# Smaller feed-forward units for the first block, a mean square in halves, a new order of loads, and a new load model in the scheduler of a fused attention and SwiGLU kernel

## The chip, the cores and the metric

The kernel runs on one core of a Trainium2 chip. The metric is the device time of one execution in microseconds (us). Each group of runs times the kernel before beside the kernels under test on the same chip. A ratio is the mean time of one kernel's fast runs over that of the other kernel's fast runs of the same rounds, so it is not quite the ratio of the medians quoted beside it. Its 95% interval is in brackets.

## The reference

Sliding-window attention (128 positions and 4 sink positions) over 4 batches, 8 heads, 768 positions, head size 64. Then each of the 3072 tokens goes through a root mean square normalisation and a SwiGLU feed-forward network (FFN).

```python
keep = is_sink | ((rel >= 0) & (rel < window))            # n_sink 4, window 128
a = softmax(where(keep, q @ k.T / sqrt(D), -1e9))
x = (a @ v).transpose(0, 2, 1, 3).reshape(B * S, H * D)   # 3072 x 512
xn = x / sqrt(mean(x * x, -1) + 1e-6) * rms_g
g = xn @ w_gate                                           # 512 x 1536
out = (g * sigmoid(g) * (xn @ w_val)) @ w_out             # 1536 x 512
```

## The kernel before

The tokens form 24 blocks of 128 rows; four blocks form a group. The 1536 FFN columns are 12 tiles of 128, called weight tiles here; "gate 2-3" means tiles 2 and 3 of the gate weights, "value 2-3" the same of the value weights. All loads except three at the start go through one software queue that GpSimd issues; it casts float32 to bfloat16 on the way.

Nothing is issued in program order. Each operation is registered with a cost in ns, what it needs and what it gives. A list scheduler (`Plan.run`) plays a model of the engines, the PSUM banks and the loads, and emits instructions in the order in which they start there. (PSUM is the memory that TensorE writes its products to; a bank is a piece of it that a product holds until it has been read.) Each engine then executes in that order and waits at the head of its queue.

```python
def land(self, ring, first, work):          # the scheduler's model of a load
    r = self.rings
    if ring == "POOL":                      # software queue
        begin = max(first, r["POOL"], r["HW"])
        r["POOL"] = begin + (1.4 * work if begin < 8500 else work)
        self.loads -= 1
        return r["POOL"] + 520
    if ring == "HW":                        # two float32 blocks and the gains, from SyncE
        begin = max(first, r["HW"])
        r["HW"] = begin + (1.25 * work if begin > 2500 else work)
        return r["HW"] + 900
    # ... transposes and stores cut
```

```python
LOADS = ("q-1 k-1 v-0 w-0-2 v-1 qkv-2 qkv-3 w-2-4 w-4-6 w-6-8 w-8-9 w-9-12 qkv-4 "
         "wo-0-6 qkv-5 wo-6-12 qkv-6 qkv-8 qkv-7")      # one literal in the source
LOADS += "".join(f" qkv-{g}" for g in range(9, NB))
WARM = 30             # products of zeros that fill TensorE's gaps
PE_MASKS = 2          # blocks masked by a product on TensorE, not on VectorE
CHUNKS = (4, 2, 2)    # group 0: one block of rows at a time, 4 weight tiles a unit

def square(g):        # mean square of a block, one ScalarE instruction
    nc.scalar.activation(out=sq, in_=T["x16", g].rearrange("p h d -> p (h d)"),
        func=ACT.Square, scale=1.0 / math.sqrt(DM), accum_out=T["ms", g])

def ffn(G, n, fts, cols, prio):             # one unit; banks and most needs cut
    pe(864, lambda: mms(bank(("g", key)), wg, G, fts, cols), ...)   # gate product
    pe(864, lambda: mms(bank(("v", key)), wv, G, fts, cols), ...)   # value product
    act(480, lambda: tanh(key), ...)
    dve(600, lambda: silu(key), ...)
    dve(605, lambda: hidden(key, G, fts, cols), ...)

for G in range(NG):
    nc_ = CHUNKS[G] if G < len(CHUNKS) else 1
    w, n = GN // nc_, 0
    for c in range(nc_):
        for ft in range(0, FTN, nc_):
            ffn(G, n, range(ft, ft + nc_), slice(c * w, (c + 1) * w), p0 + 10 * n)
            n += 1
```

The softmax here doesn't subtract the row's maximum and nothing guards it: scores larger than these inputs give would overflow.

Of the kernel before, what the change touches and what calls it, by code (L numbers as in the profile page):

```python
# [9 lines left out]
ALU = mybir.AluOpType  # L10
ACT = mybir.ActivationFunctionType
FP32 = mybir.dt.float32
# [14 lines left out]
class Plan:  # L27
# [3 lines left out]


    LATE = 300
    HOP = {"PE": 40, "ACT": 35, "DVE": 35, "POOL": 90, "SP": 60}
    START = {"PE": 800, "ACT": 800, "DVE": 1030, "POOL": 1290, "SP": 800}

# [5 lines left out]
    def op(self, ways, needs=(), gives=(), prio=0.0, takes=(), drops=(), ring=None, work=0.0,  # L42
# [3 lines left out]
            drops=tuple(drops), ring=ring, work=work, mode=mode, at=len(self.ops), ready=0,  # L46
        ))

    def land(self, ring, first, work):


        r = self.rings
        if ring == "POOL":
            begin = max(first, r["POOL"], r["HW"])
            r["POOL"] = begin + (1.4 * work if begin < 8500 else work)
            self.loads -= 1
            return r["POOL"] + 520
        if ring == "HW":
            begin = max(first, r["HW"])
            r["HW"] = begin + (1.25 * work if begin > 2500 else work)  # L60
            return r["HW"] + 900
        begin = max(first, r["TR"], r["POOL"])
        if self.loads:
            r["POOL"] = max(r["POOL"], first) + work
            work *= 2
        r["TR"] = begin + work
        return r["TR"] + (350 if ring == "TR" else 650)

    def run(self):
        free, users = dict(self.START), {}  # L70
        self.loads = sum(o["ring"] == "POOL" for o in self.ops)
        wait = {o["at"]: set(o["needs"]) for o in self.ops}
        cand = {e: [] for e in free}
        left = len(self.ops)
        for o in self.ops:
            for t in o["needs"]:
                users.setdefault(t, []).append(o)
            if not o["needs"]:
                for e in o["ways"]:
                    cand[e].append(o)  # L80
        busy, warm, mode, order = [], False, 0, []
        while left:
            first = None
            for e, found in cand.items():
                for o in found:
                    k = len(o["takes"])
                    if k > len(self.banks):
                        continue
                    ready = o["ready"] + self.HOP[e] if o["ready"] else 0
                    if k:  # L90
                        ready = max(ready, sorted(self.banks.values())[k - 1] + 40)
                    start = max(free[e], ready)
                    key = (start, o["prio"], ready, o["at"])
                    if first is None or key < first[0]:
                        first = key, e, o
            if first is None:
                raise RuntimeError("stuck: %s" % [
                    (o["gives"], list(wait[o["at"]])) for o in self.ops if o["at"] in wait
                ][:20])
            (start, *_), e, o = first  # L100
            for x in o["ways"]:
                cand[x].remove(o)
            wait.pop(o["at"])
            left -= 1
            ns, lat, fn = o["ways"][e]
            if e == "PE":
                busy = [(a, d) for a, d in busy if a > start - 3413]
                warm = start - free[e] < 4000 and (warm or sum(d for a, d in busy) > 3000)
                ns = ns if warm else 2 * ns
                if o["mode"] != mode:  # L110
                    ns, mode = ns + 110, o["mode"]
                busy.append((start, ns if mode != 2 else 0))
                lat = ns + 180
            for s in o["takes"]:
                i = min(self.banks, key=lambda i: (self.banks[i], i))
                del self.banks[i]
                self.held[s] = i
            free[e] = start + ns
            end = start + lat
            if o["ring"] is not None:  # L120
                end = self.land(o["ring"], end, o["work"]) + self.LATE
            for s in o["drops"]:
                self.banks[self.held[s]] = end + 12
            for t in o["gives"]:
                for x in users.pop(t, ()):
                    x["ready"] = max(x["ready"], end + 12)
                    w = wait[x["at"]]
                    w.discard(t)
                    if not w:
                        for way in x["ways"]:  # L130
                            cand[way].append(x)
            order.append((start, end, e, fn, o))
        return order
# [3 lines left out]
def kernel(  # L137
# [34 lines left out]
    GROW = "SP"  # L172
    CAST_DVE = 600
    MASKS_PRIO = -5
    POOL_AT = (1,2)
    DEPTH = 8
    LOADS = "q-1 k-1 v-0 w-0-2 v-1 qkv-2 qkv-3 w-2-4 w-4-6 w-6-8 w-8-9 w-9-12 qkv-4 wo-0-6 qkv-5 wo-6-12 qkv-6 qkv-8 qkv-7"
    LOADS += "".join(f" qkv-{g}" for g in range(9, NB))
    PE_MASKS = 2
    POOL_MASK_FROM = 16  # L180
    X_DMA_FROM = 9
    QK_DMA_FROM = 8
    LD = 16
    GATE_FROM = 6
    LOAD_LEAD = 9
    LEAD_FROM = 10
    WARM = 30
    GATE_LEAD = 6
    T_LEAD = 3
    SPLIT = (0,1)  # L190
    CHUNKS = (4,2,2)
    GB_PRIO = 2000

    const = ctx.enter_context(tc.tile_pool(name="const", bufs=1))
    ld = ctx.enter_context(tc.tile_pool(name="ld", bufs=LD))
# [330 lines left out]
    def normal(g, u):  # L526
# [7 lines left out]
            in1=rden.unsqueeze(2).to_broadcast((P, 4, D)), op=ALU.mult,  # L534
        )

    def square(g):
        T["ms", g] = small.tile([P, 1], FP32, name="ms")
        sq = xpool.tile([P, DM], BF16, name="sq")
        nc.scalar.activation(  # L540
            out=sq, in_=T["x16", g].rearrange("p h d -> p (h d)"), func=ACT.Square,
            scale=1.0 / math.sqrt(DM), accum_out=T["ms", g],
        )

    def rms(g):
        m = small.tile([P, 1], FP32, name="m")
        nc.vector.tensor_scalar(
            out=m, in0=T.pop(("ms", g)), scalar1=1e-6, scalar2=None, op0=ALU.add,
        )
        y = small.tile([P, 1], FP32, name="y")  # L550
        nc.vector.tensor_scalar(
            out=y.bitcast(I32), in0=m.bitcast(I32), scalar1=-0.5,
# [94 lines left out]
    for g in range(NB):  # L647
# [41 lines left out]
        for u in range(2):  # L689
# [7 lines left out]
            else:  # L697
# [12 lines left out]
            dve(548, lambda g=g, u=u: normal(g, u),  # L710
                [("av", g, u)] + ([("xr", g - 3)] if g >= 3 else [])
                + ([("n", g - 1, u)] if g else []), [("n", g, u)], early, drops=[("av", g, u)])
        act(720, lambda g=g: square(g),
            [("n", g, 0), ("n", g, 1), "table"] + ([("ms", g - 1)] if g else []), [("ms", g)],
            early)
        dve(1745, lambda g=g: rms(g),
            [("ms", g), "gb"] + ([("xt", g - 3)] if g >= 3 else [])
            + ([("xr", g - 1)] if g else []), [("xr", g)], early)
# [34 lines left out]
    def mms(ps, w_sb, G, fts, cols):  # L753
        n = cols.stop - cols.start
        for i, ft in enumerate(fts):
            for kt in range(KTN):
# [2 lines left out]
                    rhs=T["xnt", G][:, kt, cols], start=(kt == 0), stop=(kt == KTN - 1),  # L759
                )  # L760

    def tanh(key):
        T["th", key] = spool.tile([P, 512], BF16, name="th")
        nc.scalar.activation(  # L764
            out=T["th", key], in_=BANK[("g", key)], func=ACT.Tanh, scale=0.5,
        )

    def silu(key):
        T["p1", key] = spool.tile([P, 512], BF16, name="p1")
        nc.vector.scalar_tensor_tensor(  # L770
            out=T["p1", key], in0=T.pop(("th", key)), scalar=1.0, in1=BANK.pop(("g", key)),
            op0=ALU.add, op1=ALU.mult,
        )

    def hidden(key, G, fts, cols):
        n, hk = len(fts), ("h", G, fts[0] // 4)
        if hk not in T:
            T[hk] = hpool.tile([P, 4, GN], BF16, name="hT")
        i = fts[0] % 4
        nc.vector.tensor_tensor(  # L780
            out=T[hk][:, i:i + n, cols],
            in0=T.pop(("p1", key)).rearrange("p (n c) -> p n c", n=n),
            in1=BANK.pop(("v", key)).rearrange("p (n c) -> p n c", n=n), op=ALU.mult,
        )

    def project(G, tb, i):
# [45 lines left out]
    def ffn(G, n, fts, cols, prio):  # L832
        key = (G, fts[0], cols.start)
        xs = [("xt", g) for g in range(G * GB + cols.start // P, G * GB + cols.stop // P)]
        before = [("h", keys[-3])] if len(keys) >= 3 else []
        keys.append(key)
        pe(864, lambda: mms(bank(("g", key)), wg, G, fts, cols),
           xs + [("wg", ft) for ft in fts], [("g", key)], prio, takes=[("g", key)])
        pe(864, lambda: mms(bank(("v", key)), wv, G, fts, cols),
           [("g", key)] + [("wv", ft) for ft in fts], [("u", key), ("F", G, n)], prio - 0.5,  # L840
           takes=[("v", key)])
        act(480, lambda: tanh(key), [("g", key), "table"] + before, [("th", key)])
        dve(600, lambda: silu(key), [("th", key)] + before, [("p1", key)], drops=[("g", key)])
        dve(605, lambda: hidden(key, G, fts, cols), [("p1", key), ("u", key)]
            + ([("O", G - 2, i) for i in range(GB)] if G >= 2 else []),
            [("h", key)], drops=[("v", key)])

    for G in range(NG):
# [1 line left out]
        nc_ = CHUNKS[G] if G < len(CHUNKS) else 1  # L850
        w, n = GN // nc_, 0
        for c in range(nc_):
            for ft in range(0, FTN, nc_):
                ffn(G, n, range(ft, ft + nc_), slice(c * w, (c + 1) * w), p0 + 10 * n)
                n += 1
        mine = [key for key in keys if key[0] == G]
        for tb in range(GB if G < NG - 1 else GB - 1):
# [61 lines left out]
```

## Time and profile before

| | before |
|---|---|
| median of 3 runs | 246.89 us (246.82 to 247.07) |
| span of the profiled execution | 244.3 us (that run took 245.98 us, the fastest of its group) |
| TensorE (PE) busy | 232.6 us, 95% |
| VectorE / ScalarE busy | 183.7 / 131.2 us |
| granted TensorE clock, mean | 0.999 |

The page of the kernel before. The first line is busy time with its share of the span and the number of instructions, by engine. The others divide the span into 40 slices of about 6 us: each digit is the busy share of a slice in tenths, and GB/s is what the DMA engines moved.

```profile
PE 232.6 (95%) x2098; PEld 147.8 (61%) x2120; DVE 183.7 (75%) x482; ACT 131.2 (54%) x276; POOL 88.8 (36%) x114
...
PE   4978999999999999999999999999999999999994
...
GB/s 112 172 170 195 192 188 188 156 146 174 171 196 130 156 124 179 142 216 133 149 35 107 133 107 86 3 21 108 120 34 21 4 21 107 86 3 0 0 86 86
```

TensorE is short of full only in the first, third and fourth slice and in the last; the loads run at a steady 170 to 195 GB/s from the second slice to the seventh. After the fourth slice the engine is dense. What can be won is TensorE work done earlier in the first 25 us.

The timeline of TensorE around the first FFN products (kernel before; columns: start us, length us, engine, line, operation, output and inputs, shapes, count; in brackets the idle time just before it and what ended it):

```profile
18.14 0.61 PE L757 MATMUL g<-xnt,wg 128*128 128x128 bf16 x8
19.75 0.62 PE L757 MATMUL g<-xnt,wg 128*128 128x128 bf16 x8 [1.00 <-DMA wg<-in_moe_w_gate_dram]
...
20.49 1.06 PE L757 MATMUL v<-xnt,wv 128*128 128x128 bf16 x16
...
22.09 1.06 PE L757 MATMUL g<-xnt,wg 128*128 128x128 bf16 x16
22.98 1.06 PE L757 MATMUL v<-xnt,wv 128*128 128x128 bf16 x16
23.88 0.61 PE L757 MATMUL g<-xnt,wg 128*128 128x128 bf16 x8
24.68 0.51 PE L757 MATMUL g<-xnt,wg 128*128 128x128 bf16 x6 [0.19 <-DMA wg<-in_moe_w_gate_dram]
```

Eight gate products run at 18.14. Then TensorE stands for 1.00 us until gate 2-3 has landed. From 19.75 it works almost without a gap.

### The profile page before, as it was taken

What the parts mean: (1) busy time and instruction counts of PE and PEld (TensorE: products, weight loads), DVE (VectorE), ACT (ScalarE), POOL (GpSimd) and SP (SyncE); (2) the same over time, 40 slices, a digit from 0 to 9 for tenths busy, and PEclk for the clock granted to TensorE, in tenths of its full rate; (3) what the DMA queues carried; (4) which work ended last, traced back from release to release, by engine and by line L of the source; (5) the groups of instructions that cost most, each with busy time, mean ns of one, the idle gap of its engine ahead of it and who ended that gap; (6) DMA issues with size and microseconds to landing.
All of it is one profiled execution on the core that took longest, in us unless ns stands there. A gap on an engine that the chain in (4) does not pass through costs nothing.

```text
span 244.3 us, 5510 instructions
## 1 busy us (share of the span) xinstructions
PE 232.6 (95%) x2098; PEld 147.8 (61%) x2120; DVE 183.7 (75%) x482; ACT 131.2 (54%) x276; POOL 88.8 (36%) x114
## 2 busy tenths in 40 slices
PE   4978999999999999999999999999999999999994
PEld 2557996875789765688875444444545544444443
DVE  4388979979899998899888499991299992377700
ACT  3886466778675837654537555735745521333111
POOL 8995755695444749423004200302504200000000
PEclk9999999999999999999999999999999999999999
DMA  8999999999999999999944544014311013200022
GB/s 112 172 170 195 192 188 188 156 146 174 171 196 130 156 124 179 142 216 133 149 35 107 133 107 86 3 21 108 120 34 21 4 21 107 86 3 0 0 86 86
DMA packets 111979, 27.22 MB, mean 111 GB/s; under 512 B 102097, under 2 KB 109009, under 8 KB 111954
## 3 DMA queue, kind: packets, MB, share of 16 engines
q0 software_dynamic: 80704, 13.90, 81.0%
q1 hardware_dynamic: 31106, 12.85, 27.0%
q8 instruction: 16, 0.26, 0.5%
q10 hardware_dynamic: 144, 0.13, 0.2%
q14 instruction: 9, 0.07, 0.1%
HBM read 28.31 MB, written 6.29 MB: 142 GB/s over the span
## 4 chain that ended last, share of the span: by engine, by line
PE 77%; DVE 9%; POOL 5%; DMA 4%; issue 3%; ACT 0%; POOLq 0%; DVEq 0%; ACTq 0%
PE o L790 23%; PE g L757 21%; PE v L757 21%; PE s L456 4%; DMA wg<-in_moe_w_gate_dram 4%; DVE hT L780 2%; PE av L520 2%; DVE p L770 2%; PE av L515 2%; DVE r L560 2%; POOL v L327 1%; DVE xr L564 1%; PE av L505 1%; PE o_last L808 1%; DVE x L532 1%
## 5 line engine op out<-in xcount | busy, mean ns | idle before, releaser
L757 PE MATMUL g<-xnt,wg 128*128 128x128 bf16 (+2 forms) x525 | 69.8, 282 | 1.6 <-DMA wg<-in_moe_w_gate_dram 1.2
L757 PE MATMUL v<-xnt,wv 128*128 128x128 bf16 (+2 forms) x522 | 71.0, 281 | 0.3
L764 ACT ACTIVATE th<-g 128x512 bf16<-128x512 f32 x72 | 42.9, 600 | 46.7 <-PE g L757 45.2
L790 PE MATMUL o<-wo,hT 128*128 128x512 bf16 x263 | 62.6, 379 | 1.2 <-issue 0.6
L770 DVE SCALAR_TENSOR_TENSOR p<-th,g 128x512 bf16<-128x512 bf16 x72 | 48.1, 683 | 16.6 <-ACT th L764 16.2
L757 PEld LDWEIGHTS <-wg 128*128 128x128 bf16 x528 | 43.1, 98 | 21.0 <-DMA wg<-in_moe_w_gate_dram 1.5
L757 PEld LDWEIGHTS <-wv 128*128 128x128 bf16 x528 | 42.6, 98 | 18.5 <-issue 0.8
L469 ACT ACTIVATE e<-s 128x512 bf16<-128x512 f32 (+1 forms) x104 | 48.4, 542 | 6.6 <-PE s L456 6.3
L780 DVE TENSOR_TENSOR hT<-p,v 128x512 bf16<-128x512 bf16 x72 | 47.2, 682 | 1.5 <-PE v L757 0.6
L790 PEld LDWEIGHTS <-hT 128*128 128x128 bf16 x276 | 25.6, 98 | 28.7 <-issue 1.3
L491 POOL TENSOR_SCALAR_AFFINE_SELECT e<-e 128x512 bf16<-128x512 bf16 x14 | 9.4, 680 | 61.8 <-ACT e L469 48.8
L798 ACT ACTIVATE osb<-o 128x512 f32<-128x512 f32 x23 | 13.8, 599 | 29.0 <-PE o L790 29.0
L323 POOL DMA_DIRECT2D k<-in_k_dram x23 | 20.5, 890 | 15.9 <-DMA v<-in_v_dram 7.0
L323 POOL DMA_DIRECT2D q<-in_q_dram x23 | 20.5, 893 | 13.0 <-DMA k<-in_k_dram 3.8
L327 POOL DMA_DIRECT2D v<-in_v_dram x24 | 21.3, 889 | 10.0 <-DMA q<-in_q_dram 6.0
L532 DVE TENSOR_TENSOR x<-av,rden 128x256 bf16<-128x256 f32 x48 | 20.4, 425 | 1.7
L540 ACT ACTIVATE sq<-x 128x512 bf16<-128x512 bf16 x24 | 15.2, 632 | 9.4 <-DVE x L532 9.3
L531 DVE RECIPROCAL rden<-av 128x4 f32<-128x4 f32 x48 | 8.5, 177 | 15.4 <-PE av L520 15.3
L486 DVE TENSOR_TENSOR e<-e,masks 128x1024 bf16<-128x1024 bf16 (+1 forms) x30 | 18.9, 650 | 1.0 <-ACT e L469 0.8
L564 DVE SCALAR_TENSOR_TENSOR xr<-x,r,gb 128x512 bf16<-128x512 bf16 x24 | 19.0, 790 | 0.9
L520 PE MATMUL av<-v,e 128*128 128x65 bf16 x192 | 16.9, 194 | 0.0
L515 PE MATMUL av<-v,e 128*128 128x65 bf16 x160 | 15.0, 193 | 0.0
(70 smaller groups left out, 177.2 us busy)
## 6 DMA issues: line engine op xcount, KB each, us to landing
out_dram<-osb SPq DMA_DIRECT2D x23, 256.0 KB, 2.2
v<-in_v_dram POOLq DMA_DIRECT2D x24, 128.0 KB, 10.4
q<-in_q_dram POOLq DMA_DIRECT2D x23, 128.0 KB, 10.9
k<-in_k_dram POOLq DMA_DIRECT2D x23, 128.0 KB, 10.8
wo<-in_moe_w_out_dram POOLq DMA_DIRECT2D x2, 768.0 KB, 12.0
wg<-in_moe_w_gate_dram POOLq DMA_DIRECT2D x4, 256.0 KB, 7.8
wv<-in_moe_w_val_dram POOLq DMA_DIRECT2D x4, 256.0 KB, 8.2
wg<-in_moe_w_gate_dram POOLq DMA_DIRECT2D x1, 384.0 KB, 9.4
```

What stands on the lines that cost most here:

```text
L323: nc.gpsimd.dma_start(out=T[name, g], in_=block_of(src, g))
L327: nc.gpsimd.dma_start(out=V16[b][:, t, :, 0:D], in_=block_of(v, g))
L469: nc.scalar.activation(out=T["e", g, u][:, 2 * hi:2 * hi + 2, n0:n1, :].rearrange("p x n c -> p x (n c)"), in_=ps.rearrange("p (j c) -> p ...
L515: nc.tensor.matmul(out=dest, lhsT=T["e", g - 1, u][:, x, 1, :], rhs=V16[b][:, t - 1, h, :], start=(t == 1), stop=False, skip_group_check=True,
L520: nc.tensor.matmul(out=dest, lhsT=T["e", g, u][:, x, 0, :], rhs=V16[b][:, t, h, :], start=(t == 0), stop=True, skip_group_check=True,)
L532: nc.vector.tensor_tensor(out=T["x16", g][:, 4 * u:4 * u + 4, :], in0=pvv[:, :, 0:D], in1=rden.unsqueeze(2).to_broadcast((P, 4, D)), op=AL ...
L564: nc.vector.scalar_tensor_tensor(out=T["xr", g], in0=T.pop(("x16", g)).rearrange("p h d -> p (h d)"), scalar=r[:, 3:4], in1=gb, op0=ALU.mu ...
L757: nc.tensor.matmul(out=ps[:, i * n:(i + 1) * n], lhsT=w_sb[:, kt, ft * P:(ft + 1) * P], rhs=T["xnt", G][:, kt, cols], start=(kt == 0), sto ...
L764: nc.scalar.activation(out=T["th", key], in_=BANK[("g", key)], func=ACT.Tanh, scale=0.5,)
L770: nc.vector.scalar_tensor_tensor(out=T["p1", key], in0=T.pop(("th", key)), scalar=1.0, in1=BANK.pop(("g", key)), op0=ALU.add, op1=ALU.mult,)
L780: nc.vector.tensor_tensor(out=T[hk][:, i:i + n, cols], in0=T.pop(("p1", key)).rearrange("p (n c) -> p n c", n=n), in1=BANK.pop(("v", key)) ...
L790: nc.tensor.matmul(out=BANK[("o", G, tb)], lhsT=T["h", G, ft // 4][:, ft % 4, tb * P:(tb + 1) * P], rhs=wo[:, ft, :], start=(ft == 0), sto ...
```

## The change

The intent: start the FFN of block 0 as soon as two weight tiles are there, shorten the path from attention to normalised rows for blocks 0 and 1, and let the scheduler model hardware and software loads as sharing the DMA engines. Several settings of the scheduler move with it, among them the order and sizes of the loads and the number of warm-up products.

```diff
-            begin = max(first, r["POOL"], r["HW"])
-            r["POOL"] = begin + (1.4 * work if begin < 8500 else work)
+            begin = max(first, r["POOL"])
+            self.soft = min(self.soft, begin)
+            r["POOL"] = self.end(begin, work, ((r["HW"], 0.25), (7000, 0.7)))
 ...
-            begin = max(first, r["HW"])
-            r["HW"] = begin + (1.25 * work if begin > 2500 else work)
+            begin = max(first + (300 if r["HW"] else 0), r["HW"])
+            r["HW"] = self.end(begin, work, ((self.soft, 1.05), (1e9, 0.38)))
 ...                       (a SLACK table of zeros, which changes nothing, cut)
-    POOL_AT = (1,2)
+    POOL_AT = (0,1)
-    LOADS = "q-1 k-1 v-0 w-0-2 v-1 qkv-2 qkv-3 w-2-4 w-4-6 w-6-8 w-8-9 w-9-12 qkv-4 wo-0-6 qkv-5 wo-6-12 qkv-6 qkv-8 qkv-7"
+    LOADS = "q-1 k-1 v-0 v-1 qkv-2 w-0-2 qkv-3 w-2-4 w-4-6 w-6-9 w-9-10 w-11-12 w-10-11 qkv-4 wo-0-6 qkv-5 wo-6-12 qkv-8 qkv-7 qkv-6"
-    PE_MASKS = 2
+    PE_MASKS = 3
-    GATE_FROM = 6
+    GATE_FROM = 7
-    LEAD_FROM = 10
-    WARM = 30
+    LEAD_FROM = 9
+    WARM = 0
+    FIRST = 2
+    SQ2 = 2
-    GB_PRIO = 2000
+    GB_PRIO = -970
 ...
+    def square_half(g, u):        # for blocks 0 and 1; rms() adds the two halves
+        cols = slice(u * DM // 2, (u + 1) * DM // 2)
+        nc.scalar.activation(
+            out=T["sq", g][:, cols], in_=T["x16", g].rearrange("p h d -> p (h d)")[:, cols],
+            func=ACT.Square, scale=1.0 / math.sqrt(DM), accum_out=T["ms", g][:, u:u + 1],
+        )
 ...                       (unit size and its costs passed through ffn, cut)
-            for ft in range(0, FTN, nc_):
-                ffn(G, n, range(ft, ft + nc_), slice(c * w, (c + 1) * w), p0 + 10 * n)
+            k = min(nc_, FIRST) if G == 0 and c == 0 else nc_
+            for ft in range(0, FTN, k):
+                ffn(G, n, range(ft, ft + k), slice(c * w, (c + 1) * w), p0 + 10 * n)
```

In `LOADS`, `w-6-9` is one load of weight tiles 6 to 8 for the gate and one for the value weights. `FIRST` is the number of weight tiles in a unit of block 0 (a unit is the gate and the value product of some tiles for some rows, with the steps behind them), and `SQ2` the number of blocks whose mean square is taken in halves. `GB_PRIO` moves the product that spreads the gains forward; `POOL_AT` places two small setup operations on GpSimd; `GATE_FROM` and `LEAD_FROM` say from which block on attention and loads are held back.

More of the change, by code (lines that the diff above doesn't have):

```diff
@@ L33 @@
     LATE = 300
+    SLACK = {"PE": 0, "DVE": 0, "ACT": 0}
     HOP = {"PE": 40, "ACT": 35, "DVE": 35, "POOL": 90, "SP": 60}
@@ L47, in op, with end @@
         ))
+    @staticmethod
+    def end(t, work, rates):
+        for until, rate in rates:
+            if t < until:
+                if work <= (until - t) * rate:
+                    return t + work / rate
+                work -= (until - t) * rate
+                t = until
+        return t + work
     def land(self, ring, first, work):
@@ L70, in run @@
         free, users = dict(self.START), {}
+        self.soft = 1e9
         self.loads = sum(o["ring"] == "POOL" for o in self.ops)
@@ L82, in run @@
         while left:
-            first = None
+            first, near = None, {}
             for e, found in cand.items():
@@ L92, in run @@
                     start = max(free[e], ready)
+                    near.setdefault(e, []).append((start, o["prio"], ready, o["at"], o))
                     key = (start, o["prio"], ready, o["at"])
@@ L100, in run @@
             (start, *_), e, o = first
+            start, _, _, _, o = min(
+                (x for x in near[e] if x[0] <= start + self.SLACK.get(e, 0)),
+                key=lambda x: (x[1], x[0], x[2], x[3]),
+            )
             for x in o["ways"]:
@@ L535, in normal @@
         )
+    def square_half(g, u):
+        if u == 0:
+            T["ms", g] = small.tile([P, 2], FP32, name="ms2")
+            T["sq", g] = xpool.tile([P, DM], BF16, name="sq")
+        cols = slice(u * DM // 2, (u + 1) * DM // 2)
+        nc.scalar.activation(
+            out=T["sq", g][:, cols], in_=T["x16", g].rearrange("p h d -> p (h d)")[:, cols],
+            func=ACT.Square, scale=1.0 / math.sqrt(DM), accum_out=T["ms", g][:, u:u + 1],
+        )
     def square(g):
@@ L546, in rms @@
         m = small.tile([P, 1], FP32, name="m")
-        nc.vector.tensor_scalar(
-            out=m, in0=T.pop(("ms", g)), scalar1=1e-6, scalar2=None, op0=ALU.add,
-        )
+        ms = T.pop(("ms", g))
+        if g < SQ2:
+            nc.vector.scalar_tensor_tensor(
+                out=m, in0=ms[:, 0:1], scalar=1e-6, in1=ms[:, 1:2], op0=ALU.add, op1=ALU.add,
+            )
+        else:
+            nc.vector.tensor_scalar(
+                out=m, in0=ms, scalar1=1e-6, scalar2=None, op0=ALU.add,
+            )
         y = small.tile([P, 1], FP32, name="y")
@@ L712 @@
                 + ([("n", g - 1, u)] if g else []), [("n", g, u)], early, drops=[("av", g, u)])
-        act(720, lambda g=g: square(g),
-            [("n", g, 0), ("n", g, 1), "table"] + ([("ms", g - 1)] if g else []), [("ms", g)],
-            early)
+        before = [("ms", g - 1)] if g else []
+        if g < SQ2:
+            for u in range(2):
+                act(512, lambda g=g, u=u: square_half(g, u),
+                    [("n", g, u), "table"] + (before if u == 0 else [("ms", g, 0)]),
+                    [("ms", g)] if u else [("ms", g, 0)], early)
+        else:
+            act(720, lambda g=g: square(g), [("n", g, 0), ("n", g, 1), "table"] + before,
+                [("ms", g)], early)
         dve(1745, lambda g=g: rms(g),
@@ L760, in mms @@
                 )
+    SIZE = {}
+    size_of = SIZE.get
     def tanh(key):
-        T["th", key] = spool.tile([P, 512], BF16, name="th")
+        n = size_of(key)
+        T["th", key] = spool.tile([P, 512], BF16, name="th")[:, 0:n]
         nc.scalar.activation(
-            out=T["th", key], in_=BANK[("g", key)], func=ACT.Tanh, scale=0.5,
+            out=T["th", key], in_=BANK[("g", key)][:, 0:n], func=ACT.Tanh, scale=0.5,
         )
     def silu(key):
-        T["p1", key] = spool.tile([P, 512], BF16, name="p1")
+        n = size_of(key)
+        T["p1", key] = spool.tile([P, 512], BF16, name="p1")[:, 0:n]
         nc.vector.scalar_tensor_tensor(
-            out=T["p1", key], in0=T.pop(("th", key)), scalar=1.0, in1=BANK.pop(("g", key)),
-            op0=ALU.add, op1=ALU.mult,
+            out=T["p1", key], in0=T.pop(("th", key)), scalar=1.0,
+            in1=BANK.pop(("g", key))[:, 0:n], op0=ALU.add, op1=ALU.mult,
         )
@@ L782, in hidden @@
             in0=T.pop(("p1", key)).rearrange("p (n c) -> p n c", n=n),
-            in1=BANK.pop(("v", key)).rearrange("p (n c) -> p n c", n=n), op=ALU.mult,
+            in1=BANK.pop(("v", key))[:, 0:size_of(key)].rearrange("p (n c) -> p n c", n=n),
+            op=ALU.mult,
         )
@@ L836, in ffn @@
         keys.append(key)
-        pe(864, lambda: mms(bank(("g", key)), wg, G, fts, cols),
+        SIZE[key] = len(fts) * (cols.stop - cols.start)
+        size = SIZE[key]
+        pe(1.6875 * size, lambda: mms(bank(("g", key)), wg, G, fts, cols),
            xs + [("wg", ft) for ft in fts], [("g", key)], prio, takes=[("g", key)])
-        pe(864, lambda: mms(bank(("v", key)), wv, G, fts, cols),
+        pe(1.6875 * size, lambda: mms(bank(("v", key)), wv, G, fts, cols),
            [("g", key)] + [("wv", ft) for ft in fts], [("u", key), ("F", G, n)], prio - 0.5,
            takes=[("v", key)])
-        act(480, lambda: tanh(key), [("g", key), "table"] + before, [("th", key)])
-        dve(600, lambda: silu(key), [("th", key)] + before, [("p1", key)], drops=[("g", key)])
-        dve(605, lambda: hidden(key, G, fts, cols), [("p1", key), ("u", key)]
+        act(54 + 0.833 * size, lambda: tanh(key), [("g", key), "table"] + before, [("th", key)])
+        dve(67 + 1.042 * size, lambda: silu(key), [("th", key)] + before, [("p1", key)], drops=[("g", key)])
+        dve(72 + 1.042 * size, lambda: hidden(key, G, fts, cols), [("p1", key), ("u", key)]
             + ([("O", G - 2, i) for i in range(GB)] if G >= 2 else []),
```

## The prediction

> **What bounds the kernel now.** TensorE: the busy table gives PE 232.6 of 244.3 us. From 24.7 us it hardly stops (busy time by stretch: under 2 us idle up to 240 us). So what counts is how much real TensorE work is done before that.
>
> That front is held by the software load queue. Its landings come back to back, 0.95 us for each q, k or v block, 1.3 us for each load of two weight tiles: gate tiles 0-1 at 9.6, gate 2-3 at 19.7, value 2-3 at 20.7, gate 4-5 at 22.0, value 4-5 at 23.3, gate 6-7 at 24.6, the last at 31.3. The PE timeline shows eight gate products at 18.14, a 1.0 us wait for gate 2-3, then dense work with one gap of 0.35 us before 24.68 (gate 6-7).
>
> **What the change does.**
> 1. Units of two tiles for block 0: same matmuls (56 ns each), three more tanh, product and hidden steps, each paying some 0.07 us of fixed cost. Not critical.
> 2. Weight tiles 0-1 move behind block 2's loads; what stands before gate 2-3 is the same set, so it lands at 19.7 again. In the changed PE order the second unit's gate (tiles 2-3) stands before the first unit's value product, so again only eight gate products run early. The finer units gain nothing there.
> 3. After that, from order and landings: values done at 21.3, block 2's attention products and a transpose to 22.3, gate 4-5 to 22.7, then a wait of about 0.7 us for value 4-5. Later units find weights and banks ready (gate 6-8, now one load, at 25.4, just in time). Also 0.2 us of sink scores move behind gate 2-3. Sum: +0.7 +0.2 -0.35, about +0.6 us when block 3's last attention product ends (38.8 before).
> 4. Halved mean square: two calls of about 0.4 us for one of 0.63, the first overlapping normalisation: perhaps 0.2 us earlier, while weights are awaited anyway. Likewise the early gain product (1.1 us between two score groups) and block 2's mask on PE (+0.9 us PE in idle time, -1.3 us VectorE).
> 5. No warm-up products. The Trainium skill ("TensorE: Matmul & The Clock Gate", Part 1) says the clock halves after an idle window of about 3.4 us. The trace agrees with a cold start: four 512-column products take 1.87 us at 4.2 us, 1.02 at 11.2 us. I expect no long idle gap before 19.7, so little cost.
> 6. The first software load follows the identity mask on GpSimd, 0.3 us later; loads may land 0.1-0.3 us later. The scheduler's new load model changes only the order.
> 7. The rest keeps nearly the same order (blocks 8, 7, 6 loaded in reverse, transposes moved to match): 0 +- 0.8 us.
>
> **Prediction: 247.2 us, 80% range 245.7 to 248.9.** Faster by over 2%: 0.02; within 2%: 0.94; slower by over 2%: 0.04. A gain is bounded by the 2 us of idle after 19.7 us.
>
> **What would show it.** Gate 2-3 landing at 19.5-20.1 and PE waiting for it; a PE wait of 0.5-1 us for value 4-5 near 23 us; block 3's last attention product ending 0.2-1.2 us later than 38.8; PE idle after 40 us as before.
>
> **What would make it wrong.** Loads running faster or slower in the new order (beside the two hardware loads at the start, or as one-tile loads); a cold clock after 19.7 us, up to 1.5 us; a PSUM bank freed late because block 1's tanh and product steps queue behind block 0's; stalls at blocks 6-8 if reverse loading misses its transposes.

## More of the kernel before

The landing of each load can be read from its semaphore's increments in the trace: a load has landed when the last of its 16 pieces has reported. In us:

```
load                    before    changed
gate 0-1                  9.59      13.43
value 0-1                11.03      14.77
gate 2-3                 19.71      18.65
value 2-3                20.65      20.92
gate 4-5                 21.96      22.03
value 4-5                23.29      23.37
gate 6-7  (changed 6-8)  24.63      25.31
value 6-7 (changed 6-8)  26.00      27.28
last gate or value load  31.34      31.75
first half of w_out      37.70      38.41
block 6, k               46.08      52.95
```

The waits of TensorE after 40 us (kernel before; columns: engine, line, what it waited for, us in total, times, longest). Waits shorter than about 0.15 us are not listed:

```profile
PE o L790 <- issue: 0.6, 4, 0.2
PE g L757 <- DVE rden L531: 0.3, 1, 0.3
```

## The result, and the profile after

| | before | changed |
|---|---|---|
| median, 4 runs each | 246.98 us (246.82 to 247.17) | 247.53 us (247.32 to 248.01) |
| ratio | | 1.0025 [1.0007, 1.0042] |
| span of the profiled execution | 244.3 us | 246.1 us |
| last TensorE product ends | 240.8 us | 242.7 us |
| block 3's last attention product starts | 38.74 us | 39.56 us |
| granted clock, mean | 0.999 | 0.998 |

The changed kernel is a quarter of a per cent slower. The two profiles overstate it: that of before is of an unusually fast run (245.98 us), that of the changed kernel of its slowest (248.01 us).

The same lines of the page, changed kernel:

```profile
PE 234.1 (95%) x2072; PEld 147.5 (60%) x2094; DVE 183.2 (74%) x484; ACT 131.7 (54%) x284; POOL 89.5 (36%) x116
...
PE   4987999989999999999999899999999999999994
...
GB/s 108 162 179 200 180 184 186 157 146 177 153 202 127 141 134 158 140 194 170 137 61 107 138 99 87 0 24 87 107 67 11 14 21 107 85 3 0 0 85 85
```

The same stretch of TensorE's timeline, changed kernel:

```profile
17.96 1.36 PE L802 MATMUL g<-xnt,wg 128*128 128x128 bf16 x16
19.25 0.29 PE L661 MATMUL ss<-qkT,ksk 128*32 128x256 bf16 x4
19.47 0.62 PE L802 MATMUL v<-xnt,wv 128*128 128x128 bf16 x8
20.96 0.62 PE L802 MATMUL v<-xnt,wv 128*128 128x128 bf16 x8 [0.88 <-ACT e L492]
...
22.35 0.61 PE L802 MATMUL g<-xnt,wg 128*128 128x128 bf16 x8
23.41 0.62 PE L802 MATMUL v<-xnt,wv 128*128 128x128 bf16 x8 [0.46 <-DMA wv<-in_moe_w_val_dram]
23.87 1.06 PE L802 MATMUL g<-xnt,wg 128*128 128x128 bf16 x16
```

There are two waits, 0.88 and 0.46 us. The profile puts the first down to an exponential on ScalarE, which ended at 20.95, 0.01 us before the product started. Value 2-3, which the product reads, landed at 20.92, 0.05 us before it. The other load waits of this trace end 0.05 us after the landing (the second one: landed 23.37, started 23.41), so the load is the likelier cause here too; in the control run below the profile itself names it (value 2-3 landed 20.65, product started 20.70, a wait of 0.70 us, the exponential done at 20.37). The second is for value 4-5, the wait that the prediction named.

The mask products and the first transpose of normalised rows show the clock and the attention chain (TensorE timeline). Kernel before, then changed:

```profile
4.16 1.87 PE L438 MATMUL s<-bias,idnos 128*128 128x512 bf16 x4 [2.07 <-DVE bias L273]
...
11.15 1.02 PE L438 MATMUL s<-bias,ident 128*128 128x512 bf16 x4
...
14.47 0.40 PE L579 MATMUL x<-ident,xr 128*128 128x128 bf16 x4 [0.67 <-DVE xr L564]
```

```profile
3.08 1.86 PE L461 MATMUL s<-bias,idnos 128*128 128x512 bf16 x4 [3.08 <-DVE bias L296]
...
9.80 1.89 PE L461 MATMUL s<-bias,ident 128*128 128x512 bf16 x4
...
16.01 1.03 PE L461 MATMUL s<-bias,ident 128*128 128x512 bf16 x4
16.87 0.39 PE L618 MATMUL x<-ident,xr 128*128 128x128 bf16 x4
```

Four mask products of 512 columns take 1.9 us at the half clock and 1.0 at the full one. The second mask runs cold at 9.80 us in the changed kernel and warm at 11.15 in the one before. The clock records agree: full from 8.4 us before, from 13.2 us in the changed kernel. Block 0's rows are transposed 2.4 us later, at 16.87 instead of 14.47.

The waits of TensorE after 40 us, changed kernel:

```profile
PE g L802 <- DMA xnt<-xr: 0.9, 1, 0.9
PE k L439 <- DMA k<-in_k_dram: 0.7, 1, 0.7
PE o L841 <- issue: 0.3, 2, 0.2
PE s L479 <- ACT qkT L446: 0.2, 1, 0.2
```

There are two waits of 0.7 and 0.9 us; the longest of the kernel before after 40 us is 0.34 us. The first is at block 6:

```profile
53.00 0.40 PE L439 MATMUL k<-ident,k 128*128 128x128 bf16 x4 [0.71 <-DMA k<-in_k_dram]
```

Block 6's k is now loaded last of blocks 8, 7 and 6; two transposes of block 8 by DMA run at the same time, and it lands at 52.95. The second is near 139 us:

```profile
139.03 1.02 PE L802 MATMUL g<-xnt,wg 128*128 128x512 bf16 x4 [0.85 <-DMA xnt<-xr]
139.89 1.03 PE L841 MATMUL o<-wo,hT 128*128 128x512 bf16 x4
...
141.10 1.03 PE L841 MATMUL o<-wo,hT 128*128 128x512 bf16 x4
```

The gate product of group 3 stands in TensorE's order ahead of eight output products. It waits for the transposed rows, while output products of 1.7 us, which read other tiles, stand behind it. This wait is not wholly new. The same place in the kernel before:

```profile
138.92 1.02 PE L757 MATMUL g<-xnt,wg 128*128 128x512 bf16 x4 [0.34 <-DVE rden L531]
```

The profile names a reciprocal, but transposed rows that this product reads landed at 138.78 us in both kernels' traces; the output products already stood in front of it there, so TensorE was idle for 0.34 us and not for 0.85. Busy time by stretch says where the difference is (columns: stretch, its length, then busy us and instructions of PE, PEld, DVE, ACT and POOL, clock, DMA share, GB/s). Kernel before, then changed:

```profile
40.00:60.00 20.00, 19.84 (x248) 14.18 (x251) 17.41 (x54) 16.01 (x37) 14.21 (x17) 1.00 2.24 165
...
120.00:150.00 30.00, 29.13 (x242) 16.96 (x244) 24.35 (x67) 16.60 (x35) 4.25 (x6) 1.00 0.58 102
```

```profile
40.00:60.00 20.00, 18.70 (x237) 13.38 (x240) 16.64 (x49) 14.73 (x34) 14.88 (x19) 1.00 2.27 167
...
120.00:150.00 30.00, 28.94 (x240) 17.46 (x243) 24.22 (x63) 16.63 (x37) 3.61 (x6) 1.00 0.67 106
```

TensorE's idle time (length less PE's busy time) is 0.16 and 0.87 us in the two stretches before, 1.30 and 1.06 us in the changed kernel. The 0.87 us of before are several smaller pieces (the longest is the 0.34 us), so the clear difference is the one at block 6. Added up from 40 to 220 us in the same way, the idle time is 1.97 us before and 3.09 us in the changed kernel: 1.1 us more.

### The profile page after: what moved, and what is told of

Read it like the earlier page. It is cut to its first block, busy times and chain, and to the rows that moved or that the text cites. A ratio compares the mean times of both kernels' runs of the same rounds, so it can differ in the third digit from the quotient of the medians.

```text
span 246.1 us, 5477 instructions
## 1 busy us (share of the span) xinstructions
PE 234.1 (95%) x2072; PEld 147.5 (60%) x2094; DVE 183.2 (74%) x484; ACT 131.7 (54%) x284; POOL 89.5 (36%) x116
## 4 chain that ended last, share of the span: by engine, by line
PE 73%; DMA 14%; POOL 8%; DVE 3%; issue 1%
PE v L802 22%; PE g L802 22%; PE o L841 20%; DMA wo<-in_moe_w_out_dram 5%; DMA wv<-in_moe_w_val_dram 5%; PE s L479 3%; DMA k<-in_k_dram 3%; POOL v L350 2%; POOL k L346 2%; PE av L543 2%; PE av L538 1%; POOL wg L392 1%; POOL q L346 1%; PE o_last L859 1%; DMA xnt<-xr 1%
## 5 line engine op out<-in xcount | busy, mean ns | idle before, releaser
L813 ACT ACTIVATE th<-g 128x512 bf16<-128x512 f32 (+1 forms) x75 | 43.3, 587 | 49.1 <-PE g L802 48.8
L841 PE MATMUL o<-wo,hT 128*128 128x512 bf16 x263 | 63.3, 380 | 0.8 <-issue 0.3
L820 DVE SCALAR_TENSOR_TENSOR p<-th,g 128x512 bf16<-128x512 bf16 (+1 forms) x75 | 48.3, 661 | 16.1 <-ACT th L813 15.6
L830 DVE TENSOR_TENSOR hT<-p,v 128x512 bf16<-128x512 bf16 (+1 forms) x75 | 47.4, 660 | 1.9 <-PE v L802 1.2
L514 POOL TENSOR_SCALAR_AFFINE_SELECT e<-e 128x512 bf16<-128x512 bf16 x14 | 8.8, 633 | 64.3 <-ACT e L492 34.3
L509 DVE TENSOR_TENSOR e<-e,masks 128x1024 bf16<-128x1024 bf16 (+1 forms) x28 | 17.5, 647 | 1.4 <-ACT e L492 1.4
L573 ACT ACTIVATE sq<-x 128x512 bf16<-128x512 bf16 x22 | 13.9, 633 | 7.7 <-DVE x L555 7.4
L543 PE MATMUL av<-v,e 128*128 128x65 bf16 x192 | 17.2, 196 | 0.2 <-ACT e L492 0.2
L543 PEld LDWEIGHTS <-e 128*128 128x128 bf16 x192 | 13.3, 99 | 3.1 <-ACT e L492 0.6
```

Of the source, the lines that this page charges most:

```text
L509: nc.vector.tensor_tensor(out=ev, in0=ev, in1=mv, op=ALU.mult)
L543: nc.tensor.matmul(out=dest, lhsT=T["e", g, u][:, x, 0, :], rhs=V16[b][:, t, h, :], start=(t == 0), stop=True, skip_group_check=True,)
L813: nc.scalar.activation(out=T["th", key], in_=BANK[("g", key)][:, 0:n], func=ACT.Tanh, scale=0.5,)
L820: nc.vector.scalar_tensor_tensor(out=T["p1", key], in0=T.pop(("th", key)), scalar=1.0, in1=BANK.pop(("g", key))[:, 0:n], op0=ALU.add, op1= ...
L830: nc.vector.tensor_tensor(out=T[hk][:, i:i + n, cols], in0=T.pop(("p1", key)).rearrange("p (n c) -> p n c", n=n), in1=BANK.pop(("v", key)) ...
L841: nc.tensor.matmul(out=BANK[("o", G, tb)], lhsT=T["h", G, ft // 4][:, ft % 4, tb * P:(tb + 1) * P], rhs=wo[:, ft, :], start=(ft == 0), sto ...
```

## The experiments

Two theories. **Theory W:** the front is held by the landing of the weights, so the units and the halves are worth nothing, and the loss lies in the loads' order and sizes. **Rivals:** U, the finer units gain and something else eats it; C, the loss is in the colder and later attention chain at the front, which follows from the missing warm-up products and the new order. All kernels gave a correct result except one.

### Block 0 in units of four tiles again

```diff
-    FIRST = 2
+    FIRST = 4
```

> The changed kernel with block 0 in units of four weight tiles again. Theory W (the front is held by the landing of the weight tiles): within 0.3 us of the changed kernel, so 247.2 to 247.9, because value tiles 2-3 land near 20.9 us whatever the unit size. Rival U (the finer units are worth something and another part of the change eats it): 0.6 us or more slower than the changed kernel, 248.1 or more.

Measured: 248.1 us (247.96 to 248.53), ratio to before 1.0056 [1.0041, 1.0070]. That lies at the edge of what U expected against the changed kernel's first median of 247.53 us, but only 0.1 us above its second (control below, 247.97). Its profile shows TensorE waiting 1.1 us for value 2-3 and then 0.7 us for block 1's transposed rows; the changed kernel fills that second gap with tiles 4-5 of block 0. So the finer units fill a gap there. Whether they gain in the total is not settled by this run, for the edit moved the later order too. Neither of the changed kernel's two late waits is in its trace, though its loads are the changed kernel's; two others stand near 62 us (waits after 60 us, longest two):

```profile
PE g L802 <- ACT xnt L624: 0.7, 1, 0.7
PE x L618 <- DVE xr L603: 0.6, 1, 0.6
```

So an edit of this kind makes the scheduler find another order, and a comparison of two such kernels compares two orders.

### One mean square call per block again

```diff
-    SQ2 = 2
+    SQ2 = 0
```

> The changed kernel with one mean square call per block again. Theory W: within 0.3 us of the changed kernel (247.2 to 247.9), since block 0's normalised rows wait for weights anyway. Rival C (the front is held by the attention chain of blocks 0 and 1, which the changed kernel finishes 2.4 us later at block 0's transpose): 0.2 to 0.5 us slower than the changed kernel.

Measured: 247.75 us (247.31 to 248.23), 1.0036 [1.0022, 1.0050], between the two measurements of the changed kernel. The halves make no difference that can be seen, as W expected.

### All loads in the old order and sizes

```diff
-    LOADS = "... v-0 v-1 qkv-2 w-0-2 qkv-3 ... w-6-9 w-9-10 w-11-12 w-10-11 ... qkv-8 qkv-7 qkv-6"
+    LOADS = "... v-0 w-0-2 v-1 qkv-2 qkv-3 ... w-6-8 w-8-9 w-9-12 ... qkv-6 qkv-8 qkv-7"
```

> The changed kernel with the load order and load sizes of before (weight tiles 0-1 early, tiles 6-7 and 8 and 9-11 as loads, blocks 6, 8, 7). Theory W: the lost time is in the loads (six one-tile loads at 0.74 us against 0.66 us a tile, the wait for value tiles 4-5, and 0.7 us for block 6's k, landed last), so 0.5 to 1.0 us faster than the changed kernel, 246.5 to 247.0. Rival C: no faster than the changed kernel, since the slow front chain stays.

Measured: 246.51 us (246.01 to 246.90), 0.9986 [0.9970, 1.0002]. The loads carried the loss: without them the changed kernel is no slower than before and perhaps a little faster. Both late waits are gone. In its profile the clock fell to half for 3.4 us in the front (columns as above):

```profile
11.10:14.50 3.40, 2.01 (x32) 1.16 (x31) 1.88 (x6) 2.27 (x9) 3.40 (x6) 1.00 2.43 155
14.50:17.90 3.40, 3.39 (x32) 2.11 (x33) 3.13 (x13) 2.35 (x7) 2.82 (x4) 0.50 1.97 175
```

### The old load model, all else changed

```diff
-            begin = max(first, r["POOL"])      # and the rest of the new model
+            begin = max(first, r["POOL"], r["HW"])
+            r["POOL"] = begin + (1.4 * work if begin < 8500 else work)
```

> The changed kernel with the old load model in the scheduler, all else changed. Theory W: the order of instructions moves a little, within 0.5 us either way of the changed kernel. If the new model is what costs: 0.5 us or more faster than the changed kernel; if it gains: 0.5 us or more slower.

Measured: 248.43 us (247.12 to 249.07), 1.0063 [1.0039, 1.0087]. That is 0.5 to 0.9 us slower than the changed kernel, but the runs scatter over 2 us. There is no sign that the new model costs anything; that it gains is possible, not shown (the intervals overlap with those of the changed kernel).

### The changed kernel again

> The changed kernel again, as the yardstick for this group: 247.3 to 248.0 us, ratio to before 1.001 to 1.005. Both theories expect the same.

Measured: 247.97 us (247.38 to 248.90), 1.0050 [1.0029, 1.0070]. The changed kernel's own two ratios, 1.0025 and 1.0050, are the uncertainty of every comparison between groups: about 0.6 us.

### Sixteen products of zeros in front

The order of everything else stays; TensorE would be idle there.

```diff
+        zeros = const.tile([P, P], BF16, name="zeros")
+        nc.vector.memset(zeros, 0.0)
+        wps = ring.tile([P, 512], FP32, name="warm", tag="bank7")
+        for _ in range(16):
+            nc.tensor.matmul(out=wps[:, 0:P], lhsT=zeros, rhs=zeros, start=True, stop=True)
```

> The changed kernel in its own order, with 16 products of zeros ahead of the first mask on TensorE, which waits there until 3.1 us anyway. Both theories expect the full clock 3 to 5 us earlier (by the lengths of the products, at about 8 to 10 us instead of 13) and block 0's transpose of normalised rows at least 1 us earlier than 16.9 us. Theory W (weights hold the front): total unchanged within 0.3 us. Rival C (the cold, late attention chain holds the front): 0.7 us or more faster, near 246.8.

Measured: 247.89 us (247.46 to 248.67), 1.0044 [1.0028, 1.0061]: unchanged. But the premise failed. The clock was full from 4.1 us, fell back from 7.5 to 10.9, and block 0's rows were transposed at 16.57 instead of 16.77 in the control, because a q of block 3 stands before them in the order. Warming up the front gained nothing; the run doesn't test rival C, whose chain it did not move.

### Old sizes and old tail, weight tiles 0-1 still behind block 2

```diff
-    LOADS = "... v-1 qkv-2 w-0-2 qkv-3 ... w-6-9 w-9-10 w-11-12 w-10-11 ... qkv-8 qkv-7 qkv-6"
+    LOADS = "... v-1 qkv-2 w-0-2 qkv-3 ... w-6-8 w-8-9 w-9-12 ... qkv-6 qkv-8 qkv-7"
```

> The changed kernel with the load sizes and the tail order (blocks 6, 8, 7) of before, but weight tiles 0-1 still behind block 2. If the loss sits in the one-tile loads and in the reversed tail: most of the 0.95 us that undoing all the loads gave, so 246.5 to 247.0. If it sits in the position of tiles 0-1: no more than 0.3 us faster than the control.

Measured: 246.29 us (245.94 to 246.56), 0.9977 [0.9962, 0.9992]. This is faster than both kernels. Its rows of block 0 are transposed at 16.83 us and its clock is full only from 13.2 us, just as in the changed kernel, so rival C falls: the late, cold chain is still there and the loss is not. The position of tiles 0-1 costs nothing either.

### Old loads and products of zeros in front

The two edits above together (all loads old).

> The changed kernel with all loads as before, and 16 products of zeros in front. The run with the loads undone fell back to the half clock from 14.5 to 17.9 us in its profile and still came to 246.5 us. If that window costs time, this is 0.3 to 0.8 us faster than that run, near 246.0, and beats both kernels; if weights alone hold the front, it stays at 246.3 to 246.7.

Measured: 246.47 us (246.11 to 246.87), 0.9983 [0.9967, 0.9998]; the run without the products had 0.9986. No gain. In its profile the clock was cold at 9.0 to 12.4 and again at 15.8 to 19.2 us, and the time was the same.

### Only the tail of the loads as before

```diff
-    ... wo-6-12 qkv-8 qkv-7 qkv-6"
+    ... wo-6-12 qkv-6 qkv-8 qkv-7"
```

> The changed kernel with only the tail of the load order as before (block 6, then 8, then 7). Tail theory: the wait for block 6's k (0.3 to 0.7 us) and the 0.9 us wait for the transposed rows near 138 us both go, total 246.3 to 246.9. If the load sizes are what costs: no more than 0.3 us faster than the changed kernel (247.3 or more).

Measured: 246.77 us (246.54 to 248.21), 1.0001 [0.9977, 1.0025], against 1.0025 and 1.0050 for the changed kernel. Waits of TensorE after 40 us (this kernel), busy time of the two stretches (this kernel, then the control), and the order near 139 us (this kernel):

```profile
PE o L841 <- issue: 0.3, 2, 0.2
PE s L479 <- ACT qkT L446: 0.2, 1, 0.2
```

```profile
40.00:60.00 20.00, 19.51 (x245) 13.75 (x247) 17.51 (x53) 15.77 (x36) 15.22 (x18) 1.00 2.15 165
...
120.00:150.00 30.00, 29.79 (x239) 17.02 (x241) 23.98 (x66) 17.09 (x37) 4.25 (x6) 1.00 0.71 112
```

```profile
40.00:60.00 20.00, 19.13 (x242) 13.63 (x245) 16.91 (x51) 15.05 (x35) 14.51 (x18) 1.00 2.17 168
...
120.00:150.00 30.00, 28.92 (x239) 17.27 (x241) 24.62 (x64) 16.62 (x37) 3.61 (x6) 1.00 0.64 104
```

```profile
137.38 1.90 PE L841 MATMUL o<-wo,hT 128*128 128x512 bf16 x8
...
139.47 1.03 PE L802 MATMUL g<-xnt,wg 128*128 128x512 bf16 x4
```

Both late waits are gone. The gate product now stands behind the output products. Block 3's last attention product starts at 39.40 us, as in the control (39.31), and TensorE's last product ends at 241.1 instead of 242.3 us. TensorE's idle time from 40 to 220 us is 1.61 us against 2.73 in the control. So 1.1 to 1.2 us came back after 40 us in the traces, from three words of the load order; both profiles are of runs near the fastest of their six. In time the gain is 0.6 us against the changed kernel's first measurement, where the intervals overlap, and 1.2 us against the second, where they just do not.

### Only the sizes of tiles 6 to 11 as before

```diff
-    ... w-6-9 w-9-10 w-11-12 w-10-11 ...
+    ... w-6-8 w-8-9 w-9-12 ...
```

> The changed kernel with only the load sizes of weight tiles 6 to 11 as before (6-7, 8, 9-11). Sizes theory: the first output weights land 0.3 to 0.5 us earlier and the total is 0.3 to 0.6 us faster than the changed kernel. Tail theory: within 0.3 us of it, and the 0.9 us wait near 138 us stays.

Measured: 247.47 us (246.97 to 247.71), 1.0017 [0.9998, 1.0036]. The last gate and value load landed at 31.06 (31.50 in the control), but the first half of w_out at 38.25, not earlier than there (37.84), and TensorE ended at 242.3 us in both. The median is 0.1 to 0.5 us below the changed kernel's: unclear. The 0.9 us wait near 138 us went, against the expectation: from 120 to 150 us TensorE is idle 0.21 us here and 1.08 us in the control. Yet that did not show at the end (its profile is of its slowest run, that of the control of its second fastest). The waits for block 6's q and k stayed (0.3 us each; idle from 40 to 60 us is 1.05 us against 0.87), as expected of the tail.

### Half of the gate and value bytes (wrong)

```diff
-                out=w_sb[:, :, cols], in_=src[:, :, cols]),
+                out=w_sb[:, 0:2, cols], in_=src[:, 0:2, cols]),
-                    ps[...], lhsT=w_sb[:, kt, ft * P:(ft + 1) * P],
+                    ps[...], lhsT=w_sb[:, kt % 2, ft * P:(ft + 1) * P],
```

> A wrong result on purpose: the changed kernel in its own order, but gate and value loads bring only the first half of the contraction rows and every product uses those. Theory W (loads hold the front): value tiles 2-3 land about 2.5 us earlier, both waits for value tiles (0.7 to 0.9 and about 0.5 us) and the wait for block 6's k vanish, total 1.2 to 2.0 us below the changed kernel, 245.7 to 246.5. If loads do not hold the front: within 0.4 us of the changed kernel. The 0.9 us wait near 138 us should stay either way, if it comes from the order and not from the loads.

Measured: 244.6 us (243.80 to 244.94), 0.9899 [0.9878, 0.9921]. The result is wrong as intended (relative error 1.2). Same order, same products; only the loads are shorter. Value 2-3 landed at 17.20 us and no TensorE wait for a load is listed any more. The waits after 40 us:

```profile
PE g L802 <- DMA xnt<-xr: 0.9, 1, 0.9
PE o L841 <- issue: 0.3, 2, 0.2
PE s L479 <- ACT qkT L446: 0.2, 1, 0.2
```

Theory W holds in kind: loads hold the front. Its size was too small: 3.1 us below the mean of the changed kernel's two medians, where 1.2 to 2.0 were expected. The front gave 2.3 us (block 3's last attention product at 37.04 against 39.31 in the control), more than the listed waits; the difference and the rest after 40 us, where block 6's k is no longer waited for, were not itemised. The 0.9 us wait near 139 us (at 135.6 here) stays with these shorter loads, so it comes from the emitted order and not from the landing of a load.

### The best kernel with units of four tiles

The edit of the 0.9977 run, and `FIRST = 4`.

> The best kernel so far (changed kernel with the load sizes and tail of before, 246.29 us, ratio 0.9977) with block 0 in units of four again. If the finer units gain 0.5 us or more here as they seemed to in the changed kernel: 246.8 or more. If that difference came only from the order the scheduler then happened to find: 246.0 to 246.6.

Measured: 246.98 us (246.84 to 247.15, five fast runs; with the slow one the median is 247.02), 1.0002 [0.9984, 1.0021] against 0.9977 [0.9962, 0.9992] with units of two, so about 0.6 us slower; the intervals just overlap and the two were measured in different groups. The profiled execution (348.62 us, clock 0.664) was slow, so it is left out and its trace proves nothing. With the first experiment this makes it possible that the finer units gain some tenths of a microsecond, or that the scheduler found a better order with them; rival U is neither shown nor ruled out.

## Why the prediction was right or wrong

The total was right: 247.2 us predicted, 247.53 and 247.97 measured, inside 245.7 to 248.9 and within 2%. Where the time goes was right only for a part, so that the number came so close is partly luck: the prediction put its loss at the front and none after 40 us. In the traces TensorE lost time after 40 us too, and undoing the load sizes and the tail, which leaves weight tiles 0-1 late and the clock cold in the front, took the whole loss away (0.9977).

- **Loads hold the front: right, and shown.** Halving the weight bytes at an unchanged order took 3.1 us off. Not shown is that nothing else could be overlapped better.
- **Step 1, smaller steps "not critical": nothing contradicts it.** In the changed kernel's trace a product step of 256 columns takes 414 ns on VectorE and one of 512 columns 682, so doing it in two halves costs about 0.15 us more; for tanh on ScalarE (394 and 603 ns) about 0.19 us.
- **Step 2, "it lands at 19.7 again ... only eight gate products run early": wrong in detail.** Gate 2-3 landed at 18.65, because in the trace of before its last piece came 2.4 us after its first and in the changed kernel 1.3 us after. So 16 gate products and eight value products were through before 20.1 us. It did not help, since value 2-3 still landed at 20.92. The same step's "the finer units gain nothing there" stays open (about 0.6 us in the best kernel between two groups, not settled in the changed one).
- **Step 3, +0.6 us at block 3's last attention product: right in the sum, in part by luck.** The wait for value 4-5 was 0.46 us instead of 0.7, and in place of the 1.00 us wait for gate 2-3 there was one of 0.88 us for value 2-3. The gap that the prediction counts as -0.35 is listed as 0.19 us. The sum was +0.8 us (39.56 against 38.74), and +0.6 in the control (39.31). All this is measured against the one trace of before, whose run was 0.8 us or more faster than its group; what a usual run of before has there was not seen. With only the tail undone the product comes just as late (39.40), and the kernel takes no longer than before.
- **Step 4, halves worth nothing on this path: right** (1.0036 without them, 1.0025 and 1.0050 with).
- **Step 5, no warm-up products at little cost: right in time, wrong in what it foresaw.** The clock came 4.8 us later and block 0's rows 2.4 us later, but warming up changed nothing (1.0044 against 1.0050) and the best kernel runs just as cold.
- **Step 7, "nearly the same order ... 0 +- 0.8 us": the step that failed.** Loading blocks 8, 7, 6 in reverse, together with the other sizes, made the scheduler choose an order with a new wait of 0.3 to 0.7 us for block 6's k and a longer one near 139 us (0.9 us instead of 0.3). TensorE was to be idle after 40 us "as before"; it was idle 1.1 us longer (3.09 against 1.97). The prediction had named the stall at block 6 as a risk, without giving it time. The second wait goes when the tail or the sizes alone are undone; the first goes with the tail and stays, at 0.3 us, with the sizes. Both also go with units of four, which bring other waits, so they belong to the order that the scheduler finds and not to the load list alone. Undoing the tail alone brings the kernel back to before (1.0001) and TensorE's end 1.2 us forward. "Transposes moved to match" was not enough: block 6's k lands at 52.95 us, beside block 8's transposes, after the place that the order gives it, so the scheduler must have expected it earlier (its own times were not recorded). And it placed a gate product ahead of ready output products.
- **The bound on a gain ("2 us of idle after 19.7 us") was not broken:** the best kernel is 0.2% faster than before. (From 25 to 240 us the busy time by stretch leaves 2.1 us idle.) It holds for this change and not for the front as such: with half of the weight bytes, at a wrong result, the kernel ran 1.0% or 2.5 us faster than before.

In short: in this change, the sizes and the tail of the loads together cost 1.0 to 1.8 us (shown: 0.9986 and 0.9977 without them, 1.0025 and 1.0050 with them). Of this the tail alone is about 0.6 to 1.2 us, by ratios whose intervals partly overlap and by the traces. All the rest together comes out even with before or slightly better. That the two late waits are the loss is read from the traces, not shown by a run that removes them at an unchanged order.

What stays open: how much the one-tile loads cost on their own, how much the finer units and the new load model gain on their own (each is near the 0.6 us by which groups differ), and why the trace of before was slow in the last piece of gate 2-3.

## What to carry to other kernels

In a kernel whose order a scheduler fixes ahead of time, read the order around every load, at the end as well as at the start: a setting far from the intended change (here three block names in a load list) can cost more than the change gains. Since a small edit can reorder everything that follows, an experiment that keeps the order says more than one that lets the scheduler run again. When an engine stands idle, look at what is ready behind the instruction that waits, not only at what it waits for. Shorten the suspected loads at an unchanged order, even with a wrong result, before making compute steps finer: it says how much a front can give. And take the profile of a run of usual length: here that of before came from a run at least 0.8 us faster than the rest of its group, which blurs every comparison of the two traces.

## What the Trainium skill lacked or had wrong

- "TensorE: Matmul & The Clock Gate", Part 1, gives a busy window as the way to the full clock and an idle window of about 3.4 us as the way back; a later section advises against idle gaps over about 3 us. In three runs here the clock fell back after windows that were partly busy. With the old loads TensorE was busy 2.01 of 3.40 us (11.10 to 14.50, longest listed gap 0.83 us) and was at half clock in the next window, although it was busy 3.39 of 3.40 us there. With products of zeros in front it was busy 1.83 of 3.41 us (4.09 to 7.50, longest gap 1.58 us) and fell to half. The page tells of short, frequent idles that make the clock oscillate ("A second HAM failure mode"), but gives no share of busy time that suffices. Busy time as the profile counts it does not decide here: with old loads and products of zeros the clock fell back after a window with 2.65 of 3.41 us busy (5.57 to 8.98), while in the changed kernel it stayed full through a stretch of 3.42 us with 2.09 busy (20.06 to 23.48). Its window length of 3413 ns is confirmed: each cold stretch between two full ones lasted 3.413 us.
- The same page advises keeping TensorE busy to reach the full clock. That is true of the clock and not of the time here: the runs that were cold 4.8 us longer lost nothing that could be measured (0.9977 for the fastest of them).
- "DMA: Bandwidth & Descriptors", section "Bandwidth", gives times by size of a single transfer, but none for casting loads that stand back to back in the software queue. Here loads of 256, 512 and 768 KB (float32 read) followed each other every 0.745 us (one weight tile), 1.33 us (two) and 1.97 us (three); a q, k or v block, 256 KB in rows of 256 bytes, took about 0.95 us. Worked out, that is 352, 394, 399 and 276 GB/s of reads. So the rate rose with the size, and was lowest for the short rows, though the queue did not run dry.
- "DMA: Bandwidth & Descriptors", "Issuing engines are not separate DMA queues", says that all issuers share the 16 DMA engines, but not what sharing costs. The trace fits: block 6's k, with two DMA transposes of another block in flight, landed 1.7 us after the q in front of it, where others follow after 0.95 us.
